# Routed attention and experts on one core: the first tiles' places moved among the products with v of the last turn but one, the first pair's preparation reordered, one transposition ahead of weights' sums

## The chip, the cores and the metric

The kernel runs on one core of one Trainium2 chip. The metric is the device time of one execution in microseconds; the kernel before takes 699.37 us (median of three runs, 699.08 to 699.43). The profile shows one execution with a span of 698.3 us and a mean granted TensorE clock of 0.990.

Five engines matter here. In the profile PE is TensorE's matmuls and PEld its weight loads, DVE is VectorE, ACT is ScalarE, POOL is GpSimd, and SP is the engine that issues most loads.

## The reference

An attention block in which a query sees only the keys of its own cluster, and then a layer of eight experts in which each row goes to one expert.

```python
# attention: q, k, v are (4, 8, 768, 64), centroids (8, 16, 64)
q_n = q / (norm(q) + 1e-06); k_n = k / (norm(k) + 1e-06); c_n = centroids / (norm(centroids) + 1e-06)
q_assign = argmax(einsum('bhsd,hcd->bhsc', q_n, c_n)); k_assign = argmax(einsum('bhsd,hcd->bhsc', k_n, c_n))
scores = scale * matmul(q, k.T)
scores = where(q_assign[..., :, None] == k_assign[..., None, :], scores, -1e9)
attn = exp(scores - max); attn = attn / (sum(attn) + 1e-09)
x = (attn @ v) as rows of 512, 3072 of them
# experts: w_gate (512, 8), w1 (8, 512, 1024), w2 (8, 1024, 512)
expert_idx = argmax(x @ w_gate, axis=1); gate_w = softmax(x @ w_gate)[expert_idx]
# rows sorted by expert; for each expert e:  y = relu(x_e @ w1[e]) @ w2[e];  out = gate_w * y
```

## The kernel before

The attention is done in 16 turns, numbered 0 to 15; a turn treats one pair of heads of one batch. A turn has 12 units: two halves of the queries by six blocks of keys. In each turn TensorE first makes the scores of all 12 units, ScalarE takes their exponentials into `A`, VectorE adds these up into `T` (the denominators), and then TensorE multiplies all 12 with v. A small scheduler hangs other jobs on points of a turn: `at(n, 4, f)` after the scores of unit 4, `at(n, mid, f)` between scores and products with v, `at(n, end, f)` after these products.

```python
def score(u):
    ps = ps_s.tile([P, 2, 512], F32, name="sps")       # three such buffers
    # 2 matmuls with qk, 2 with the one-hot clusters ohT
    A[u] = ap.tile([P, 2, HS], F32, name="A")          # 12 such buffers
    nc.scalar.activation(A[u], ps[:, :, 0:HS], AF.Exp, scale=D**-0.5)
    if j == 1:   # T = A[u-1] + A[u]
        nc.vector.scalar_tensor_tensor(T[g, half], in0=A[u - 1], scalar=1e-9 / P, in1=A[u], ...)
    elif j > 1:
        nc.vector.tensor_tensor(T[g, half], T[g, half], A[u], op=ALU.add)
# ... (cut)
for n in range(-4, NTURN + 2):
    for i, x in enumerate(range(n * NB, (n + 1) * NB)):
        if 0 <= x < NU:
            score(x)
        run(n, i)
    run(n, mid)
    for x in range(n * NB, (n + 1) * NB):
        if 0 <= x < NU:
            attend(x)                                   # products with v
    run(n, end)
```

While the last turns run, the first tiles of rows for experts 0 and 1 are placed: of the rows of the first three batches, each gets a slot (`slots1`), one-hot matrices are made from it (`one_hots1`, on VectorE and GpSimd), 18 small matmuls turn these into row numbers (`tokens1`), four more spread them over the partitions (`spread1`), and GpSimd gathers the rows (`gather1`). `n + 2` below is turn 14.

```python
n = NG - HP                                             # 16 - 4 = 12
at(n, end, choose, pl, front)
at(n + 1, mid, count, front)
at(n + 1, mid, slots1)
at(n + 1, mid, one_hots1, 0)
at(n + 1, end, one_hots1, 1)
at(n + 2, 4, tokens1)
at(n + 2, 8, spread1)
at(n + 2, 8, gather1, 0)
at(n + 3, mid, gather1, 1)
at(n + 3, mid, turn_rows1, 0)                           # L305 and L308 on VectorE
# ... (cut)
at(g, end, similar, g + 2); at(g, end, assign, g + 2)   # clusters of the turn after next
at(g, end, keep, g, 0, S); at(g + 1, mid, weigh, g)     # xb; sums' and gate's matmuls
at(NG, mid, first_half, 0, 0, FB // 4)                  # experts' first layer, from xu
```

The first pair's preparation, before turn 0: q and k are transposed on TensorE, the centroids `cn` are normalised and transposed (`blocks`, which fills `cblk`), and `similar` multiplies the two. `big` is a constant made on VectorE from an iota of GpSimd.

```python
# GpSimd: ident, cblk, first_c, first_e, wg, one_row, ohTs, then
nc.gpsimd.tensor_copy(wg[r, :, a, 0:E], wg_in[r])       # needs the load of wg_in
# VectorE: cs2, cinv, cn, and then
nc.gpsimd.iota(part_i, ...)
nc.vector.tensor_scalar(part_i, part_i, ...)            # then 5 small steps to big
# turn(0, 0): 4 transposes of q, 4 of k, copies to qk by VectorE (q) and ScalarE (k)
# blocks():   1 transpose of cn, 2 copies to cblk by VectorE
# turn(0, 1): 2 of q, 2 of k into one bank pair, one copy by ScalarE:
nc.scalar.copy(qk[g][:, :, 512:S], ps[:, 0 : 2 * n * P].rearrange("p (w s) -> p w s", w=2))
# put(0): four copies by ScalarE, four scalings by VectorE, into ohT
```

The experts' part begins with the tiles placed early; later full groups use seven products in place of eight (`sums_w1`, `sums_x` make the sums for them on VectorE).

```python
gather_of(groups[0]); adds[0](); gather_of(groups[1])
for f in sums_w1(groups[1]):                            # four sums of weights, L400 and L401
    f()
g = groups[0]
g["xT"] = p1.tile([P, DB, CAP], F32, name="xu", bufs=1)
divide_rows(g); turn_of(g)                              # L305 and L308, to xu
layer2(groups1[1])                                      # L386
layer1(g, (0, FB // 2)); layer1(g, (FB // 2, FB))       # L321, from xu
```

Of the kernel before, what the change touches and what calls it, by code (L numbers as in the profile page):

```python
# [8 lines left out]
F32 = mybir.dt.float32  # L9
BF16 = mybir.dt.bfloat16  # L10
I32 = mybir.dt.int32
AX = mybir.AxisListType.X
AF = mybir.ActivationFunctionType
ALU = mybir.AluOpType
# [6 lines left out]
NB = 12  # L21
# [164 lines left out]
def kernel(  # L186
# [243 lines left out]
    def sums_w1(g):  # L430
        t = pools["sums"].tile([P, 4, KH, F // 2], F32, name="w1s")
        g["w1s"] = [t[:, i] for i in range(4)]
        return sums_a(g["w1s"], *a_of1(g))
# [302 lines left out]
    with ExitStack() as actx:  # L736
# [55 lines left out]
        nc.scalar.dma_start(out=wg_in, in_=moe_w_gate.rearrange("(a p) e -> p a e", p=P))  # L792
        make_identity(nc, ident)
        nc.vector.tensor_copy(ident_b, ident)
        def idle(ps, n):

            for i in range(n):
                nc.tensor.matmul(ps[:, 0:P], lhsT=ident, rhs=ident, start=True, stop=True)  # L798
# [46 lines left out]
        for a in range(2):  # L845
            nc.vector.tensor_scalar(cn[:, a, :], csb, scalar1=cinv[:, 0:1], scalar2=None, op0=ALU.mult)


        part_i = consts.tile([P, 1], I32)
        nc.gpsimd.iota(part_i, pattern=[[0, 1]], base=0, channel_multiplier=1)  # L850
        nc.vector.tensor_scalar(
            part_i, part_i, scalar1=4, scalar2=1, op0=ALU.arith_shift_right, op1=ALU.bitwise_and
        )
        big = consts.tile([P, 2, 2], F32)
        nc.vector.tensor_copy(big[:, 1, 0:1], part_i)
        nc.vector.tensor_scalar_mul(big[:, 1, 0:1], big[:, 1, 0:1], BIG)
        nc.vector.tensor_scalar(big[:, 0, 0:1], big[:, 1, 0:1], scalar1=-1.0, scalar2=BIG, op0=ALU.mult, op1=ALU.add)
        for a in range(2):
            nc.vector.tensor_scalar_mul(big[:, a, 1:2], big[:, a, 0:1], -1.0)

        def blocks():
            cps = bank()
            nc.tensor.transpose(cps[:, 0:P], cn.rearrange("p a d -> p (a d)"), ident)
# [7 lines left out]
        def turn(g, piece):  # L871

            if piece == 0:
                qk[g] = qkp.tile([P, 2, S], F32, name="qk")
            n = NQ - 4 if piece else 4
            ps = wide().rearrange("p a c -> p (a c)")
            for i in range(2 * n):
                w, j = divmod(i, n)
                nc.tensor.transpose(
                    ps[:, i * P : (i + 1) * P], rows[g, "qk"[w]][:, 4 * piece + j].rearrange("p a d -> p (a d)"), ident  # L880
                )
            if piece == 0:
                apart(
                    nc.vector.tensor_copy(qk[g][:, 0, 0:512], ps[:, 0:512]),
                    nc.scalar.copy(qk[g][:, 1, 0:512], ps[:, 512:1024]),
                )
            else:
                nc.scalar.copy(qk[g][:, :, 512:S], ps[:, 0 : 2 * n * P].rearrange("p (w s) -> p w s", w=2))

        def turn_blocks(g):  # L890

# [50 lines left out]
        def places(half, a):  # L942

            return slice(half * 32, half * 32 + 32), slice(a * D, a * D + 32), slice(half * HS, (half + 1) * HS)
# [13 lines left out]

        def put(g):

            t, oh = sims.pop(g), ohTs[g % 2]
            ohT[g] = oh
            for half in range(2):
                for a in range(2):
                    i, r, cols = places(half, a)
                    k = slice(D + half * 32, D + half * 32 + 32)
                    nc.scalar.copy(oh[r, 0, cols], t[i])
                    nc.vector.tensor_scalar(
                        oh[r, 1, cols], t[k], scalar1=big[k, a, 0:1], scalar2=big[k, a, 1:2], op0=ALU.mult, op1=ALU.add
                    )  # L970


        A, T, O = {}, {}, {}
# [6 lines left out]
        def score(u):  # L980
            g, half, j = where(u)
            qs = slice(half * HS, (half + 1) * HS)
            ks = slice(j * P, (j + 1) * P)
            ps = ps_s.tile([P, 2, 512], F32, name="sps")
            for a in range(2):
                r = slice(a * D, (a + 1) * D)
                nc.tensor.matmul(ps[:, a, 0:HS], lhsT=qk[g][r, 1, ks], rhs=qk[g][r, 0, qs], start=True, stop=False)  # L987
            for a in range(2):
                r = slice(a * D, (a + 1) * D)
                nc.tensor.matmul(ps[:, a, 0:HS], lhsT=ohT[g][r, 1, ks], rhs=ohT[g][r, 0, qs], start=False, stop=True)  # L990
            A[u] = ap.tile([P, 2, HS], F32, name="A")
            nc.scalar.activation(A[u], ps[:, :, 0:HS], AF.Exp, scale=D**-0.5)  # L992
            if j == 1:
                T[g, half] = tp_.tile([P, 2, HS], F32, name="T", bufs=4)
                nc.vector.scalar_tensor_tensor(
                    T[g, half], in0=A[u - 1], scalar=1e-9 / P, in1=A[u], op0=ALU.add, op1=ALU.add
                )
            elif j > 1:
                nc.vector.tensor_tensor(T[g, half], T[g, half], A[u], op=ALU.add)  # L999

        def attend(u):
            g, half, j = where(u)
            if j == 0:
                O[g, half] = ps_o.tile([P, 512], F32, name="O")
            a_ = A.pop(u)
            for a in range(2):
                nc.tensor.matmul(  # L1007
                    O[g, half][a * D : (a + 1) * D, 0:HS], lhsT=rows[g, "v"][:, a, j, :], rhs=a_[:, a, :],
                    start=(j == 0), stop=(j == NQ - 1),
                )  # L1010
# [92 lines left out]
        def at(n, part, f, *a):  # L1103
            jobs.setdefault((n, part), []).append((f, a))
# [7 lines left out]
        at(3, end, place_consts2)  # L1112
        at(-4, mid, turn, 0, 0)
        at(-4, mid, load_next)
        at(-4, mid, blocks)
        at(-4, end, turn, 0, 1)
        at(-3, mid, similar, 0)
        at(-3, mid, assign, 0)
        at(-3, mid, assign2, 0)
        at(-3, mid, put, 0)  # L1120
        at(-2, end, idle_of, 20)
        at(-1, end, turn_blocks, 1)
        for f in (similar, assign, assign2):
# [62 lines left out]
        n = NG - HP  # L1186
        at(n, end, choose, pl, front)
        at(n + 1, mid, count, front)
        at(n + 1, mid, slots1)
        at(n + 1, mid, one_hots1, 0)  # L1190
        at(n + 1, end, one_hots1, 1)
        at(n + 2, 4, tokens1)
        at(n + 2, 8, spread1)
        at(n + 2, 8, gather1, 0)
        at(n + 3, mid, gather1, 1)
        at(n + 3, mid, turn_rows1, 0)

# [32 lines left out]
        def run(n, part):  # L1230
            for f, a in jobs.get((n, part), ()):
                f(*a)
# [4 lines that stand above are left out]
                    score(x)  # L1237
                run(n, i)
            run(n, mid)
            for x in range(n * NB, (n + 1) * NB):  # L1240
                if 0 <= x < NU:
                    attend(x)
            run(n, end)


# [86 lines left out]
    def turn_of(g):  # L1332
        if "xT" not in g:
            g["xT"] = pools["wk"].tile([P, DB, CAP], F32, name="xgT")
        turn_rows(g)
# [31 lines left out]
    adds[0]()  # L1367
    gather_of(groups[1])
    groups[0]["w"], groups[1]["w"] = weights[1], w_s
    for f in sums_w1(groups[1]):  # L1370
        f()
    g = groups[0]
    g["xT"] = p1.tile([P, DB, CAP], F32, name="xu", bufs=1)
    divide_rows(g)
    turn_of(g)
    layer2(groups1[1])
    gather_of(groups[2])
    groups[2]["xT"] = p1.tile([P, DB, P], F32, name="xT2", bufs=1)
# [107 lines left out]
```

## Time and profile before

| | busy | share of the span |
|---|---|---|
| PE | 676.6 us | 97% |
| PEld | 439.3 us | 63% |
| DVE | 471.8 us | 68% |
| ACT | 310.8 us | 45% |
| POOL | 250.1 us | 36% |

The page of the profile has busy times by engine, the span in 40 slices of 17.46 us, the chain of work that ended last, and groups of instructions. Apart from the page the trace answers questions: who waited for whom, the instructions in order of time, and busy times by stretches. In a line of the timeline stand the start, the duration, the engine, the line of the kernel, the operation, what it writes and reads, and in brackets how long the engine was idle before it and what released it. Matmuls of float32 stand there in two records each. The turns 12, 13, 14 and 15 start their scores at 251.97, 271.79, 292.01 and 321.38 us of the span, and the experts' first layer starts at 341.38 us.

### The profile page before, as it was taken

The numbers are of one execution on the slowest core, as the hardware profiler recorded it, in microseconds if no ns is written. First come the engines' busy times: TensorE is split into PE (matmuls) and PEld (weight loads), VectorE is DVE, ScalarE is ACT, GpSimd is POOL, SyncE is SP. The second block draws the span as 40 slices with busy tenths as digits, with TensorE's granted clock in tenths as the row PEclk, the third lists the DMA queues.
The fourth block names the chain that finished last, engine by engine and source line by source line (L and its number), as shares of the span: only waits on it lengthen the run. The fifth ranks groups of instructions, "written<-read, shape, count | busy, mean of one in ns | idle before, by whom it ended". The sixth has DMA issues, their size and how long they took to land.

```text
span 698.3 us, 11976 instructions
## 1 busy us (share of the span) xinstructions
PE 676.6 (97%) x4603; PEld 439.3 (63%) x4603; DVE 471.8 (68%) x739; ACT 310.8 (45%) x470; POOL 250.1 (36%) x327
## 2 busy tenths in 40 slices
PE   8999999999999999879999999999999999999994
PEld 6454444444454444445666679878798787888761
DVE  5997788778897778985656558666765767554300
ACT  3888777777887777658111022212112111131100
POOL 4022222211222222138605773737353463313101
PEclk9999999999999999989999999999999999999997
DMA  7667774986869652412245259766775866768540
GB/s 141 90 92 104 139 151 86 164 158 125 138 72 174 92 91 23 51 24 56 42 124 170 51 181 303 275 236 215 256 272 178 299 202 243 256 213 309 162 138 20
DMA packets 149538, 106.71 MB, mean 153 GB/s; under 512 B 115553, under 2 KB 119649, under 8 KB 149474
## 3 DMA queue, kind: packets, MB, share of 16 engines
q1 hardware_dynamic: 135266, 77.41, 43.6%
q0 software_dynamic: 8640, 19.63, 13.5%
q10 hardware_dynamic: 5568, 8.83, 4.1%
q8 instruction: 38, 0.62, 0.4%
q14 instruction: 26, 0.21, 0.1%
HBM read 93.06 MB, written 13.30 MB: 152 GB/s over the span
## 4 chain that ended last, share of the span: by engine, by line
PE 70%; issue 15%; POOL 6%; DVE 5%; DMA 1%; ACT 0%; ACTq 0%; POOLq 0%; DVEq 0%
PE sps L987 17%; PE O L1007 16%; PE sps L321 9%; PE sps L498 8%; PE sps L386 6%; PE sps L520 5%; PE sps L990 4%; POOL xg L292 3%; POOL out_dram L341 2%; PE sps L1029 2%; DVE T L999 2%; PE sps L908 2%; PE sps L357 1%; DMA xg<-x_rows,g_idx 1%; PE sps L798 1%
## 5 line engine op out<-in xcount | busy, mean ns | idle before, releaser
L992 ACT ACTIVATE A<-sps 128x768 f32<-128x768 f32 x192 | 153.5, 812 | 32.4 <-PE sps L990 28.6
L987 PE MATMUL sps<-qk 64*128 64x384 f32 x768 | 159.9, 495 | 2.7 <-DVE sim L915 2.2
L292 POOL DMA_INDIRECT xg<-x_rows,g_idx x104 | 115.7, 1113 | 122.4 <-DVE xgT L308 82.4
L999 DVE TENSOR_TENSOR T<-T,A 128x768 f32<-128x768 f32 x128 | 122.7, 959 | 13.0
L1007 PE MATMUL O<-A,v_in 128*64 128x384 f32 x768 | 127.4, 488 | 0.0
L987 PEld LDWEIGHTS sps<-qk 64*128 64x128 f32 x768 | 68.1, 189 | 53.3 <-issue 43.1
L1007 PEld LDWEIGHTS O<-A,v_in 128*64 128x64 f32 x768 | 53.7, 137 | 67.7 <-issue 65.9
L990 PE MATMUL sps<-ohT 64*128 64x384 bf16 x384 | 64.0, 326 | 0.0
L341 POOL DMA_INDIRECT out_dram<-zo,s_idx x32 | 38.5, 1204 | 69.4 <-ACT zo L337 30.7
L386 PE MATMUL sps<-w,h_sb 128*128 128x512 f32 x144 | 63.1, 592 | 0.0
L321 PEld LDWEIGHTS sps<-xgT,w 128*128 128x128 f32 x448 | 51.0, 192 | 3.7 <-issue 3.7
L321 PE MATMUL sps<-xgT,w 128*128 128x128 f32 x448 | 51.3, 275 | 0.0
L1041 POOL COPY dens<-ls 128x12 f32<-128x12 f32 x16 | 3.7, 232 | 127.7 <-DVE ls L1037 127.7
L1060 POOL DMA_DIRECT2D x_rows<-xb x68 | 48.3, 719 | 2.0 <-issue 0.5
L386 PEld LDWEIGHTS sps<-w,h_sb 128*128 128x128 f32 x144 | 26.8, 190 | 30.6 <-issue 30.6
L926 POOL TENSOR_TENSOR sim<-sim,first_c 128x384 f32<-128x384 f32 x14 | 14.0, 1003 | 87.8 <-DVE sim L925 87.8
L955 ACT ACTIVATE ohT<-ohs,big 32x384 bf16<-32x384 bf16 x60 | 42.0, 700 | 0.8
L364 ACT COPY zc<-sps 32x512 f32<-32x512 f32 x24 | 13.9, 579 | 60.2 <-PE sps L357 60.0
L498 PEld LDWEIGHTS sps<-xs,w1s 128*128 128x128 f32 x288 | 36.0, 190 | 5.0 <-DVE xs L409 4.2
L337 ACT COPY zo<-sps 128x512 f32<-128x512 f32 x12 | 7.0, 586 | 71.0 <-PE sps L386 65.2
L498 PE MATMUL sps<-xs,w1s 128*128 128x144 f32 x288 | 37.9, 288 | 0.0
L331 ACT ACTIVATE h_sb<-sps 128x512 f32<-128x512 f32 (+1 forms) x18 | 9.6, 578 | 60.2 <-PE sps L321 60.2
(261 smaller groups left out, 949.6 us busy)
## 6 DMA issues: line engine op xcount, KB each, us to landing
w<-in_moe_w_dram SPq DMA_DIRECT2D x28, 2048.0 KB, 9.2
w<-in_moe_w_dram ACTq DMA_DIRECT2D x16, 512.0 KB, 4.5
v_in<-in_v_dram SPq DMA_DIRECT2D x16, 384.0 KB, 3.8
q_in<-in_q_dram SPq DMA_DIRECT2D x60, 96.0 KB, 4.2
k_in<-in_k_dram SPq DMA_DIRECT2D x60, 96.0 KB, 5.6
x_rows<-xb POOLq DMA_DIRECT2D x60, 96.0 KB, 6.1
xg<-x_rows,g_idx POOLq DMA_INDIRECT x104, 3.5
x_rows<-pad SPq DMA_DIRECT2D x64, 3.0 KB, 2.2
```

Of the source, the lines that this page charges most:

```text
L292: nc.gpsimd.indirect_dma_start(out=g["xg"][:, n, :], out_offset=None, in_=x_q[0 : 4 * g["rows"], :], in_offset=bass.IndirectOffsetOnAxis(a ...
L321: nc.tensor.matmul(o, lhsT=g["w"][0][:, c, fb * P : (fb + 1) * P], rhs=g["xT"][:, c, :cols], start=(c == 0), stop=(c == DB - 1),)
L341: ins = nc.gpsimd.indirect_dma_start(out=out[:, :], out_offset=bass.IndirectOffsetOnAxis(ap=g["si"](j)[0:m], axis=0), in_=zo[0:m], in_offs ...
L386: nc.tensor.matmul(zp, lhsT=g["h"][:, fb, j * P : (j + 1) * P], rhs=g["w"][1][:, fb, :], start=(fb == 0), stop=(fb == FB - 1),)
L498: nc.tensor.matmul(o, lhsT=a[:, c, f * P : (f + 1) * P], rhs=b[:, c, :], start=(c == 0), stop=(c == KH - 1),)
L955: nc.scalar.activation(ohT[g][r, 1, cols], t[k], AF.Identity, scale=big[k, a, 0:1], bias=big[k, a, 1:2])
L987: nc.tensor.matmul(ps[:, a, 0:HS], lhsT=qk[g][r, 1, ks], rhs=qk[g][r, 0, qs], start=True, stop=False)
L990: nc.tensor.matmul(ps[:, a, 0:HS], lhsT=ohT[g][r, 1, ks], rhs=ohT[g][r, 0, qs], start=False, stop=True)
L992: nc.scalar.activation(A[u], ps[:, :, 0:HS], AF.Exp, scale=D**-0.5)
L999: nc.vector.tensor_tensor(T[g, half], T[g, half], A[u], op=ALU.add)
L1007: nc.tensor.matmul(O[g, half][a * D : (a + 1) * D, 0:HS], lhsT=rows[g, "v"][:, a, j, :], rhs=a_[:, a, :], start=(j == 0), stop=(j == NQ - 1),)
L1060: nc.gpsimd.dma_start(out=x_d[b * S + c0 : b * S + c1, quad, hp * 32 : (hp + 1) * 32].rearrange("(n t) d -> t n d", t=32), in_=xb[quad * 3 ...
```

## The change

It moves work of the last turns, of the start and of one place among the experts.

- The places: `slots1` and both `one_hots1` come after the products with v of turn 13, and so behind `similar` and `assign` of turn 15. `tokens1`, `spread1` and the first gather come among the products with v of turn 14, after the fourth and the ninth of the 12. To have VectorE free for them, the sums into `T` of units 3 to 11 of turn 14 are put off until after the gather's indices. The aim is that TensorE need not stand for the placing.
- The start: `big` is made first; `blocks` comes between the transposes of q and of k; the copy of the second piece is split between VectorE and ScalarE; two of ScalarE's four copies in `put` come after two exponentials of turn 0.
- The experts: the division and transposition of the first group's rows come before the four sums of weights of the next group.

The core of the diff, with cuts:

```diff
+        part_i = consts.tile([P, 1], I32)      # moved up with big, ahead of idle, cblk, ..., cn
+        nc.gpsimd.iota(part_i, pattern=[[0, 1]], base=0, channel_multiplier=1)
 # ... (cut)
+                if i == n and piece == 0:
+                    blocks()
                 nc.tensor.transpose(
-                    ps[:, i * P : (i + 1) * P], rows[g, "qk"[w]][:, 4 * piece + j]. ...
+                    ps[:, w * 512 + j * P : w * 512 + (j + 1) * P], rows[g, "qk"[w]][:, 4 * piece + j]. ...
             else:
-                nc.scalar.copy(qk[g][:, :, 512:S], ps[:, 0 : 2 * n * P].rearrange("p (w s) -> p w s", w=2))
+                for w, copy in enumerate((nc.vector.tensor_copy, nc.scalar.copy)):
+                    copy(qk[g][:, w, 512:S], ps[:, w * 512 : w * 512 + n * P])
 # put: the copies of the second half are put_q(0, 1)
+        at(0, 1, put_q, 0, 1)
 # score:
+            if g == NG - 2 and u % UG >= 3:
+                later_sums.append((u, A[u]))
+            else:
+                add_up(u, A[u])
 # ... (cut)
-        at(n + 1, mid, slots1)
-        at(n + 1, mid, one_hots1, 0)
+        at(n + 1, end, slots1)
+        at(n + 1, end, one_hots1, 0)
         at(n + 1, end, one_hots1, 1)
-        at(n + 2, 4, tokens1)
-        at(n + 2, 8, spread1)
-        at(n + 2, 8, gather1, 0)
+        at(n + 2, UG + 3, tokens1)
+        at(n + 2, UG + 8, spread1)
+        at(n + 2, UG + 8, gather1, 0)
+        at(n + 2, UG + 8, sums_of_later)
 # ... (cut)
-            for x in range(n * NB, (n + 1) * NB):
+            for i, x in enumerate(range(n * NB, (n + 1) * NB)):
                 if 0 <= x < NU:
                     attend(x)
+                run(n, NB + i)
 # ... (cut), the experts:
-    for f in sums_w1(groups[1]):
-        f()
     g = groups[0]
     g["xT"] = p1.tile([P, DB, CAP], F32, name="xu", bufs=1)
     divide_rows(g)
     turn_of(g)
+    for f in sums_w1(groups[1]):
+        f()
     layer2(groups1[1])
```

## The prediction

> **What bounds the kernel now.** I began with the page: busy shares and the span in slices.
>
> ```profile
> PE   8999999999999999879999999999999999999994
> DVE  5997788778897778985656558666765767554300
> PEclk9999999999999999989999999999999999999997
> ```
>
> TensorE is full nearly everywhere; only the first slice and slices 17 and 18 (279 to 314 us) are not, and the granted clock dips there too. So time is to be had only where TensorE stands or runs slowly. Who it waited for, over the whole span:
>
> ```profile
> PE sps L691 <- POOL oh_c L681: 3.4, 1, 3.4
> PE sps L987 <- DVE sim L915: 2.2, 1, 2.2
> PE sps L908 <- DVE cblk L866: 1.7, 1, 1.7
> PE sps L321 <- DVE xu L308: 1.5, 1, 1.5
> ...
> PE sps L987 <- DVE tv L700: 0.4, 1, 0.4
> ```
>
> The change aims at all five. Turn 13 beside turn 14, by busy times in stretches (length, PE, PEld, DVE, ACT, POOL, clock, DMA share, GB/s), with a stretch after the long wait:
>
> ```profile
> 271.79:292.01 20.22, 20.22 (x158) 10.14 (x156) 18.68 (x31) 15.37 (x22) 4.70 (x8) 1.00 0.48 43
> 292.01:321.38 29.37, 23.38 (x171) 11.32 (x167) 20.48 (x43) 15.04 (x21) 13.92 (x16) 0.88 0.21 40
> ...
> 304.00:306.00 2.00, 2.00 (x10) 0.91 (x8) 1.83 (x6) 0.81 (x1) 0.00 (x0) 0.50 0.02 4
> ```
>
> Turn 14 takes 9 us more than turn 13, 6 of them idle, the rest at a clock of 0.50. TensorE's timeline shows it:
>
> ```profile
> 298.68 0.38 PE L691 MATMUL sps<-oh_c,oh_r 128*128 128x8 bf16 x9
> 302.48 0.38 PE L691 MATMUL sps<-oh_c,oh_r 128*128 128x8 bf16 x9 [3.42 <-POOL oh_c L681]
> 302.79 1.65 PE L987 MATMUL sps<-qk 64*128 64x384 f32 x4
> 304.23 0.53 PE L990 MATMUL sps<-ohT 64*128 64x384 bf16 x2
> 304.55 1.49 PE L987 MATMUL sps<-qk 64*128 64x384 f32 x4
> ```
>
> After the wait a unit of scores takes 1.6 us; in turn 13 it takes 0.81.
>
> The start, from the chain that ended last:
>
> ```profile
> 7.11 0.21 POOL wg L825
> ...
> 7.38 0.14 POOL part_i L850
> ...
> 8.51 0.60 DVE qk L884
> ...
> 9.62 0.85 PE sps L908 x8
> ```
>
> The constant `big` waits for a load of the gate's weights that it doesn't need, and VectorE's copies wait behind `big`.
>
> [...] 0.50 after the 3.42 us idle, for some 5.5 us, while the wait of 2.2 us at 294 us left the clock at 1.00. [...] So I follow VectorE by adding durations in program order. [...] The two `oh_c` took 1.50 us beside VectorE's one-hots (0.75 each); for the gathers it isn't plain (1.53 and 1.71 us beside sums, 0.94 later). I use it for the range.
>
> **Part 1, the places.** Times are those of the trace before, without the earlier start.
>
> TensorE. Scores of turn 14 start at 292.01. `similar` of turn 15 is now read by VectorE at once, so its buffer is free and the 2.2 us wait goes; 12 units take 9.89 us as in turn 13 (271.79 to 281.68): 301.90. `weigh` 1.11 (chain): 303.01. Products with v are 7.89 for 12, 0.66 each; four make it 305.64. The 18 place matmuls take 2 x 0.31 (302.48 to 302.79): 306.26. Five products: 309.55; the spread 0.18; three products: turn 15 starts at about 311.7 instead of 321.38.
>
> Is the placing ready? VectorE has `cnt_f` done at 291.0, and `similar` to `ohs` takes 4.56 from 292.1 (turn 13: 271.91 to 276.47): 296.7. The slots take 3.03 (291.01 to 294.04): 299.7. Two rounds of one-hots, 1.38 (294.04 to 295.42) and 1.34 (299.97 to 301.31): 302.4. GpSimd's second pair starts after its first, 299.9 + 1.5 + 1.2 = 302.6. TensorE asks at 305.6, 3 us later: no wait. Two sums and the denominators' transpose bring VectorE to 305.2, before the place matmuls end at 306.3; `hlb` follows at once, and the spread at 309.6 finds it. So TensorE wins 321.38 - 311.7 = 9.7 us here.
>
> Not all of it stays. VectorE's indices are done at 309.75 + 1.05 = 310.8. Then come the eight postponed sums: 3.0 for three (311.81 to 314.81) and 5.1 for five (283.37 to 288.49): 318.9. That is ahead of what needs them: the exponential that reuses unit 3's buffer comes at about 315, its sum ends at 311.9; `weigh` of turn 14 is due at 311.7 + 9.89 = 321.6. `xb` takes 1.0: 319.9. The ten sums of turn 15 then run without a pause, 10.3: 330.2. TensorE has finished turn 15's products at 321.6 + 1.11 + 7.89 = 330.6, and `weigh` of turn 15 at 331.7. But the experts' first layer needs `xu`:
>
> ```profile
> 335.39 1.51 DVE L305 TENSOR_TENSOR xg<-xg 128x1152 f32<-128x1152 f32 x1
> 336.93 1.38 DVE L308 STREAM_TRANSPOSE xu<-xg 128x1152 f32<-128x1152 f32 x1
> ```
>
> From the last sum to L305 is 0.8 (334.60 to 335.39), to the end of L308 another 2.85: 330.2 + 3.65 = 333.85. TensorE waits about 2.1 us for VectorE, and its first layer starts at 333.9 instead of 341.4. **Part 1: 7.5 us**, of 9.7 that TensorE alone would give. The gathers start 1.3 us earlier, at 310.9; nine in 12.3 us and 3.5 to land put the last at about 326, in time.
>
> **Part 2, the start.** `big` moves into VectorE's free time before 3.13 us, where it waits for the centroids. `cn` is there at 6.56; its transpose follows q's and is done at 6.9, `cblk` (0.45) at 7.4. q's copy (0.68) then ends at 8.1, that of the second piece (about 0.4, from 0.68 for 512 columns) at 8.5, and `similar` starts at about 8.6 instead of 9.62: 1.0 us. The 40 idle matmuls behind it and VectorE's chain to `ohT` move with it. In turn 0 some is lost: k of turn 1, whose last load is issued at about 13.3 with 3.5 us to land, may hold VectorE until 16.8 where it could start at 16.4, and its transpose of `sim` releases TensorE at 23.14. The two postponed copies of `put` let the first exponential start 0.7 us sooner and delay the third by as much: nothing net. **Part 2: 0.8 us.**
>
> **Part 3, the sums of weights.**
>
> ```profile
> 384.00 0.68 DVE L371 TENSOR_TENSOR zo<-zc 32x512 f32<-32x512 f32 x1
> ...
> 388.13 1.22 DVE L401 TENSOR_TENSOR w1s<-w,w1s 128x1024 f32<-128x1024 f32 x1
> 390.12 0.84 DVE L308 STREAM_TRANSPOSE xu<-xg 128x640 f32<-128x640 f32 x1
> ```
>
> Four sums (384.61 to 389.26) go behind L305 and L308. The last of the five gathers is issued at 381.62, and with 3.5 us lands at 385.1, so `xu` is there at about 386.9, before TensorE is done with L386 at 389.6. Its wait of 1.5 us goes; the sums end at 391.6 and aren't read before 407. **Part 3: 1.5 us.**
>
> **The sum.** 7.5 + 0.8 + 1.5 = 9.8; 699.4 - 9.8 = 689.6 us. Behind 391 us TensorE waits for no engine, and loads of weights follow the release of their buffers by TensorE, so the gain should reach the end.
>
> **Rivals.** (a) VectorE isn't a bound: it catches up sooner than I add, or the wait for `xu` is small. Then part 1 gives up to 9.7, and the kernel takes 687.4. Against it: VectorE has no gap from 310 to 334 us in my sum. (b) The new wait is longer: sums and gathers held up by each other, rows landing after 331, or a wait for `xu` beyond 3.4 us, with the experts' first layer at half clock. A clock of 0.50 for 5.5 us costs about 2.7 us, the longer wait 1 to 2: 693 to 694. For it: VectorE's chain is tight, and the first gathers took 1.5 to 1.7 us beside sums. Against: 12.3 us for nine is measured with sums beside the first ones, and 5 us are to spare. (c) The gain is taken back among the experts by GpSimd or transfers, which the chain shows from 557 us on: 697 or more. Against it: TensorE's timeline has no gap there that an engine ended, and the matmuls end at 688.2, 10 us before the span.
>
> **Range and chances.** Prediction 689.6. (a) sets the low end, 687.4, and a mild (b) the high end, 692.0. Faster by over 2% would need 685.4, more than all the waits hold: 0.03. Slower by over 2% needs a wait nobody shows: 0.01. Within 2%: 0.96.
>
> **What would show it.** Right: the waits for `oh_c`, for `sim` at turn 14 and for `xu` of 128x640 are gone; turn 14's products and places end about 9.7 us sooner; no 0.50 clock there; one new wait of about 2 us, L321 for `xu` of 128x1152; `similar` at about 8.6. Wrong: that wait missing, or above 3.4 us with half clock after it; `weigh` of turn 14 or exponentials of turn 15 waiting for `T`; gaps in TensorE after 400 us that weren't there.

## The result, and the profile after

The changed kernel takes 693.92 us (median of four runs, 692.79 to 695.03); the kernel before, beside it, 699.23 us. The ratio is 0.9924, with a 95% interval of 0.9904 to 0.9944. A second series gave 693.07 us and 0.991 (0.9897 to 0.9923). So the change wins some 5.3 to 6.8 us of the 9.8 predicted, and the time lies above the range of 687.4 to 692.0 us.

The profile after is of the run of 692.79 us, with a span of 691.1 us. The page's slices, to set beside those of before:

```profile
PE   8999999999999999999899999999999999999994
DVE  6987788788898778879666269566765667564200
PEclk9999999999999999999999999999999999999998
```

The dent of slices 17 and 18 is gone from PE and from the clock. A smaller dent stands in slice 19 (counted from 0, 328 to 346 us). Who TensorE waited for, over the span, with the sum of the waits, their number and the longest:

```profile
PE sps L321 <- DVE xu L308: 2.0, 1, 2.0
PE sps L498 <- issue: 1.6, 1, 1.6
PE sps L811 <- POOL ident masks.py:199: 1.4, 1, 1.4
PE sps L386 <- ACT hs L331: 0.6, 1, 0.6
PE sps L911 <- POOL b1off_i L252: 0.6, 1, 0.6
PE sps L911 <- ACT A L1002: 0.4, 1, 0.4
```

The waits for `oh_c`, `sim`, `tv` and `cblk` are gone. The wait for `xu` at L321 is now the one for 128x1152 that the prediction foretold, 2.0 us for 2.1. The second line was foretold by nothing: 1.6 us at L498, put down to "issue", that is, to nothing that the profile sees.

Turn 14 from its first scores to those of turn 15, by busy times (columns as before):

```profile
292.26:312.18 19.92, 19.92 (x170) 9.98 (x167) 15.06 (x39) 14.89 (x21) 9.32 (x14) 1.00 0.23 42
```

19.92 us with no idle time and a full clock, where it was 29.37 with 6 of them idle. The first layer follows, in TensorE's timeline:

```profile
334.24 15.76 PE L321 MATMUL sps<-xu,w 128*128 128x288 f32 x64 [1.98 <-DVE xu L308]
```

It starts at 334.24 instead of 341.38, so 7.14 us have been won by then. What is missing is missing elsewhere, behind this point and at the start. Here is the new wait, in the timeline of all engines behind 390 us:

```profile
391.17 0.41 SPq L236 DMA_DIRECT2D w<-in_moe_w_dram  x1
391.17 0.49 DVE L329 TENSOR_SCALAR h_sb<-sps 128x320 f32<-128x320 f32 x1 [3.78 <-PE sps L321]
391.19 0.95 POOL L292 DMA_INDIRECT xg<-x_rows,g_idx  x1 [0.30 <-issue]
...
397.63 1.36 DVE L305 TENSOR_TENSOR xg<-xg 128x1152 f32<-128x1152 f32 x1 [5.97 <-DMA xg<-x_rows,g_idx]
...
401.49 0.73 PE L498 MATMUL sps<-xs,w1s 128*128 128x144 f32 x4 [1.64 <-issue]
```

and the same place in the kernel before:

```profile
398.01 0.95 POOL L292 DMA_INDIRECT xg<-x_rows,g_idx  x1 [0.30 <-issue]
...
400.07 0.41 SPq L236 DMA_DIRECT2D w<-in_moe_w_dram  x1
...
400.60 1.38 DVE L305 TENSOR_TENSOR xg<-xg 128x1152 f32<-128x1152 f32 x1
```

L305 divides the rows of the second group, and needs the last gather of that group (L292). Before, the gather had a start of 2.06 us on the 2 MB load of weights (L236), and its rows were there by 400.60, 2.6 us after the issue, without a wait. Now both are issued within 0.02 us, and L305 waits 5.97 us, until 6.4 us after the issue. L308 and the sums into `xs` follow (L408, L409), and TensorE's first product with `xs` comes 1.64 us late. The wait stands under "issue", but the chain to it is plain from VectorE's lines.

Why the load caught up with the gather: both come sooner than before, the load by 8.90 us and the gather by 6.82. The load waits for a buffer that TensorE's L321 releases (SyncE stands 15.7 us for it before and 14.0 after, and issues the load at 400.07 and 391.17), and L321 no longer waits for `xu`. GpSimd's gathers go on in their own order. The trigger of the load came forward by 2.08 us more than the gather that the load now disturbs.

### The profile page after: what moved, and what is told of

The parts are those of the page before. It is cut to its first block, busy times and chain, and to the rows that moved or that the text cites. A ratio compares the mean times of both kernels' runs of the same rounds, so it can differ in the third digit from the quotient of the medians.

```text
span 691.1 us, 11981 instructions
## 1 busy us (share of the span) xinstructions
PE 674.3 (98%) x4603; PEld 439.6 (64%) x4603; DVE 471.8 (68%) x740; ACT 310.7 (45%) x470; POOL 253.0 (37%) x327
## 4 chain that ended last, share of the span: by engine, by line
PE 74%; issue 14%; POOL 7%; DMA 2%; DVE 1%; ACT 1%; ACTq 0%; POOLq 0%; DVEq 0%
PE O L1034 17%; PE sps L997 17%; PE sps L321 9%; PE sps L498 8%; PE sps L386 7%; PE sps L520 5%; POOL xg L292 5%; PE sps L1000 4%; PE sps L1056 2%; POOL out_dram L341 2%; PE sps L911 2%; PE sps L357 1%; PE sps L811 1%; DMA xg<-x_rows,g_idx 1%; DMA wg_in<-in_moe_w_gate_dram 1%
## 5 line engine op out<-in xcount | busy, mean ns | idle before, releaser
L292 POOL DMA_INDIRECT xg<-x_rows,g_idx x104 | 120.0, 1154 | 116.6 <-DVE xgT L308 81.9
L997 PE MATMUL sps<-qk 64*128 64x384 f32 x768 | 157.1, 487 | 0.1
L386 PE MATMUL sps<-w,h_sb 128*128 128x512 f32 x144 | 63.1, 592 | 0.0
L321 PEld LDWEIGHTS sps<-xgT,w 128*128 128x128 f32 x448 | 51.0, 192 | 3.7 <-issue 3.7
L321 PE MATMUL sps<-xgT,w 128*128 128x128 f32 x448 | 51.3, 275 | 0.0
L386 PEld LDWEIGHTS sps<-w,h_sb 128*128 128x128 f32 x144 | 26.8, 190 | 30.6 <-issue 30.6
L498 PEld LDWEIGHTS sps<-xs,w1s 128*128 128x128 f32 x288 | 36.0, 190 | 6.7 <-DVE xs L409 4.2
L498 PE MATMUL sps<-xs,w1s 128*128 128x144 f32 x288 | 37.8, 288 | 1.6 <-issue 1.6
```

Of the source, the lines that this page charges most:

```text
L292: nc.gpsimd.indirect_dma_start(out=g["xg"][:, n, :], out_offset=None, in_=x_q[0 : 4 * g["rows"], :], in_offset=bass.IndirectOffsetOnAxis(a ...
L321: nc.tensor.matmul(o, lhsT=g["w"][0][:, c, fb * P : (fb + 1) * P], rhs=g["xT"][:, c, :cols], start=(c == 0), stop=(c == DB - 1),)
L386: nc.tensor.matmul(zp, lhsT=g["h"][:, fb, j * P : (j + 1) * P], rhs=g["w"][1][:, fb, :], start=(fb == 0), stop=(fb == FB - 1),)
L498: nc.tensor.matmul(o, lhsT=a[:, c, f * P : (f + 1) * P], rhs=b[:, c, :], start=(c == 0), stop=(c == KH - 1),)
```

## The experiments

The first theory, from the two traces: part 1 came as predicted; part 3's 1.5 us are given back by the collision of load and gather; part 2 is lost somewhere at the start; and in part of the runs the clock falls to half behind the wait for `xu`. The rivals: part 1 is worth less than it looks and the rest is as predicted; or the gain is lost in the long stretch behind 400 us (rival (c) of the prediction).

### The changed kernel once more, and each part by itself

`again` is the changed kernel without an edit.

> The changed kernel once more, to see what parts its runs, which lay at 692.8 and at 695.0 us. Theory A: the 2.2 us between them are half clock in one stage, begun by one of the two new waits of TensorE (2.0 us for xu, 1.6 us ahead of L498); a run at 695 shows a stretch of about 4 us at a clock of 0.50 right behind one of them, and mean clock 0.993 instead of 0.996. Theory B: it is the start[...]; then the idle matmuls and the transposes differ and the rest is the same. Expected: runs between 692.5 and 695.5 us, in two heaps.

Measured: 693.07 us (692.29 to 694.83). Four of the five runs lie between 692.29 and 693.41, one at 694.83: two heaps, as expected. The profile is of a run of 692.29 us and doesn't show what parts them; `no_part3` below does.

`part1_only` is the kernel before with part 1 of the diff, `put`'s copies kept together:

```diff
-        at(n + 2, 4, tokens1)
-        at(n + 2, 8, spread1)
-        at(n + 2, 8, gather1, 0)
+        at(n + 2, UG + 3, tokens1)
+        at(n + 2, UG + 8, spread1)
+        at(n + 2, UG + 8, gather1, 0)
+        at(n + 2, UG + 8, sums_of_later)
 # and the slots and one-hots of the same part
```

> The kernel before with the places' part of the change alone. Theory A: part 1 carries the whole gain, 7.0 to 7.5 us where no half clock follows the wait for xu and about 5 us where it does; the waits for oh_c and sim in turn 14 are gone, and the wait for xu of 128x1152 is 2.0 us. Rival: the three parts add up to what the changed kernel gains only together, and part 1 alone gives 4 us or less.

Measured: 692.44 us (694.2, 692.42, 692.45, 692.39) beside 699.42, ratio 0.9899 (0.9885 to 0.9913). Part 1 alone gives 7.0 us, more than the whole change in its first series. In its trace L321 starts at 333.86, 7.52 us sooner than before: the prediction's 7.5. (The profiled run of before took 700.01 us, 0.6 above its median.)

`part3_only` is the kernel before with the last part of the diff alone:

```diff
-    for f in sums_w1(groups[1]):
-        f()
     divide_rows(g)
     turn_of(g)
+    for f in sums_w1(groups[1]):
+        f()
```

> The kernel before with the sums of weights moved, and nothing else. Theory A: the wait for xu of 128x640 (1.5 us) goes, a wait of about 1.6 us ahead of L498 comes, and the time is the same within 0.4 us. Rival: the collision of load and gather comes only with the earlier turns; then this part alone brings 1.5 us.

Measured: 699.9 us, ratio 1.0006 (1.0000 to 1.0013): nothing, and by no means 1.5 us. The first lines of TensorE's waits (the places are those of before in it, with their waits):

```profile
PE sps L691 <- POOL oh_c L681: 3.4, 1, 3.4
PE sps L987 <- DVE sim L915: 2.2, 1, 2.2
PE sps L498 <- issue: 1.5, 1, 1.5
```

The wait of 1.5 us for `xu` is out of the list, and one of 1.5 us at L498 is in it. The load is issued at 398.43 and the group's last gather at 398.46, and L305 waits 5.83 us for the rows. Beside the 400.07 and 398.01 of before, the load comes 1.64 us sooner and the gather 0.45 us later: two of GpSimd's issues take 1.75 and 1.97 us beside the moved sums, where before only one took 1.94. So part 3 makes its own loss, without help from the other parts.

`no_part3` is the changed kernel with that edit taken back.

> Changed kernel with the four sums of weights ahead of the division and transposition again, as before. Theory A: part 3's 1.5 us are given back at L498, so time is the same within 0.4 us; the wait for xu of 128x640 (1.5 us) is back, and the 1.6 us ahead of L498 are gone. Rival (the wait at L498 comes from something else, part 3 is worth its 1.5 us): time rises by 1.5 us.

Measured: 693.93 us (692.46 to 695.13), ratio 0.9911 (0.9896 to 0.9925). TensorE's waits for `xu` are two again, 3.5 us together, and L498 doesn't wait. From the other side too, part 3 is worth nothing.

One stretch of the traces shows it without the scatter of the times: from L321's first product with the rows of 128x1152 to the first product of L520, a later layer. It takes 88.28 us before (341.38 to 429.66), and 88.09 in `part3_only` (341.47 to 429.56): 0.19 us won where 1.5 were predicted. From L520's first product to the end of the span the kernel before, the changed one and all eight kernels from `again` to `busy_wait` take 268.6 to 268.7 us. So the rival that the gain is lost in the long stretch behind 400 us holds for the one wait at L498 and for nothing behind 430 us.

### The load behind the gather

`load_later` is the changed kernel with the weights' load held back until the second group's last gathered rows have landed, by a transfer of one element out of them, ahead of it in the same queue:

```diff
+    held2 = pools["wk"].tile([1, 1], F32, name="held2", bufs=1)
+    nc.sync.dma_start(out=held2, in_=groups[1]["xg"][0:1, NJ * 4, DB * 32 : DB * 32 + 1])
     fetch1_of(2)
```

> Changed kernel, the load of weights for the third group kept back until the last gathered block of the second group has landed. Theory A: that load, which now starts in the same moment as the last gather's issue, keeps the rows from landing (6.4 us instead of under 2.6); kept back, the 1.6 us wait ahead of L498 goes, and time falls by 1.3 to 1.8 us against the changed kernel. Rival: the gathers are late by themselves, since GpSimd issues them beside the moved sums (1.75 and 1.96 us for two of them); then the wait stays and time changes by under 0.5 us.

Measured: 692.24 us (690.9 to 692.88), ratio 0.9894 (0.988 to 0.9909), 0.8 us less than `again` in the same series; I had expected 1.3 to 1.8 less, and the two profiled runs do differ by 1.39 us (690.9 and 692.29). L498 doesn't wait, and VectorE's L305 comes at 393.56:

```profile
390.98 0.95 POOL L292 DMA_INDIRECT xg<-x_rows,g_idx  x1 [0.30 <-issue]
...
393.56 1.38 DVE L305 TENSOR_TENSOR xg<-xg 128x1152 f32<-128x1152 f32 x1 [2.10 <-DMA xg<-x_rows,g_idx]
...
395.69 0.41 SPq L236 DMA_DIRECT2D w<-in_moe_w_dram  x1
```

That is 4 us sooner than in the changed kernel. With the load out of the way the same gather, issued 0.21 us sooner, lands 2.6 us after its issue, which shows the collision to be the cause and not only its companion. From L321's first product to L520's first it is 86.52 us (334.03 to 420.55), 1.76 less than before: without the collision part 3 gives what was predicted for it, and a little more.

### The wait for xu, and the clock behind it

The prediction has VectorE as the bound ahead of `xu`, with eight postponed sums in its way. `two_sums` lets two of the eight run earlier, behind `tokens1`:

```diff
-        def sums_of_later():
-            for x in later_sums:
+        def sums_of_later(m=NB):
+            for x in later_sums[:m]:
                 add_up(*x)
+            del later_sums[:m]
+        at(n + 2, UG + 3, sums_of_later, 2)
```

> Changed kernel, two of the eight postponed sums already between the place matmuls and the spread, where VectorE stands for 2.3 us. Theory A: VectorE sets the start of the experts' first layer, so the 2.0 us wait for xu goes almost whole and time falls by 1.7 to 2.1 us; if the half clock of the slower runs hangs on that wait, the two heaps become one as well, and the median falls by up to 3 us. Rival: the sums delay the indices and the gathers, and xu waits for its rows: no gain.

Measured: 690.66 us (690.37 to 691.78), ratio 0.9874 (0.986 to 0.9888). The first lines of TensorE's waits:

```profile
PE sps L498 <- issue: 1.6, 1, 1.6
PE sps L811 <- POOL ident masks.py:199: 1.4, 1, 1.4
PE sps L386 <- ACT hs L331: 0.6, 1, 0.6
```

The wait for `xu` is gone, and the median is 2.4 us under that of `again` for a wait of 2.0. No run lies near 695.

`both` has the edits of `two_sums` and `load_later`.

> The changed kernel with two postponed sums moved to VectorE's gap, and the load of weights kept back behind the gather. Theory A: the two gains add up, since they lie in different stages: 1.5 us below the kernel with the two sums alone, so 689.0 to 689.5 us, and neither wait is left. Rival: the kept back load comes late for its own use and costs what it brought: 690.5 us.

Measured: 689.13 us (688.86 to 689.46), ratio 0.9851 (0.9839 to 0.9864). This is the best time that was measured beside a kernel before of 699.4, 4 us under the changed kernel, and it is inside the range that the prediction gave the change. That is no confirmation of the prediction: it had counted the wait of 2 us for `xu` as staying, and `both` removes that one too.

The runs of the changed kernel fall in two heaps, some 693 and some 695. The one profile of `no_part3` is of a run of 695.13 us, and shows why, in stretches of two microseconds behind the wait of 2.0 us:

```profile
334.00:336.00 2.00, 1.16 (x4) 0.87 (x5) 0.69 (x1) 0.00 (x0) 1.70 (x2) 0.83 0.39 21
336.00:338.00 2.00, 2.00 (x6) 1.43 (x5) 0.91 (x3) 0.00 (x0) 1.39 (x3) 0.50 0.25 47
338.00:340.00 2.00, 2.00 (x9) 1.50 (x8) 1.62 (x7) 0.00 (x0) 2.00 (x3) 0.82 0.33 68
340.00:342.00 2.00, 2.00 (x10) 1.58 (x9) 0.27 (x2) 0.95 (x3) 2.00 (x5) 1.00 0.53 83
```

The granted clock is the third column from the right. It is 0.50 for some 3.5 us, behind a wait of 2.0 us; in the same stretches of the changed kernel's profile (a run of 692.79) it is 1.00:

```profile
336.00:338.00 2.00, 2.00 (x10) 1.57 (x9) 1.48 (x7) 0.00 (x0) 1.70 (x2) 1.00 0.30 68
```

Ten records of products in two microseconds instead of six. `busy_wait` tells whether it is the standing idle that does it. TensorE's wait is filled with eight products that nobody reads (`n` is NG there):

```diff
+        at(n, mid, idle_of, 8)
         at(n, mid, first_half, 0, 0, FB // 4)
```

> The changed kernel with 8 idle products of the identity (16 records, 1.9 us) ahead of the experts' first layer, so that TensorE works while it waits for xu. Theory A: the half clock behind the wait comes from standing idle; it is gone, no run lies at 695, and all runs lie between 692.2 and 693.5 us, though xu is there no sooner. Theory B (the half clock has another origin): runs at 695 stay as frequent as in the changed kernel (3 of 9 so far).

Measured: 691.2 us (690.65 to 692.31), ratio 0.9885 (0.987 to 0.9899). Its TensorE timeline:

```profile
332.19 2.05 PE L811 MATMUL sps<-ident 128*128 128x128 f32 x16
334.26 10.91 PE L321 MATMUL sps<-xu,w 128*128 128x288 f32 x44
```

L321 starts no sooner than in the changed kernel (334.26 and 334.24), yet no run lies near 695. By itself that is weak: where seven of 19 runs lie there (counted below), four without one come about by chance one time in six. With `two_sums` and `both`, where TensorE doesn't stand there at all, it is 13 runs without one, so that the standing is well supported as the cause; that idle products alone prevent the half clock is only suggested. The median is below what I expected of this kernel, for another reason: L498's wait is gone from its profile too. There the last gather was issued at 390.78, 0.4 us ahead of the load at 391.19, and L305 came at 395.52. One more of the gathers fell ahead of the sums of weights there (issued at 379.02, 0.98 us long), and so the later ones came sooner. That some tenths of a microsecond in the order of issue decide 1.6 us fits the collision, and it means that the 0.45 us by which part 3 delays the gather belong to the loss: the load's coming forward by 1.64 us alone would have left the gather a start of 0.42, as much as it has here.

### The start

`part2_only` is the kernel before with part 2 alone, `part2_again` the same kernel in another series, and `no_part2` the changed kernel without part 2.

> The kernel before with part 2 of the change alone (constants, centroids' block and copies at the start, and the two postponed copies of put). My prediction gave part 2 0.8 us: then 698.5 to 698.8 beside 699.4. The traces of the kernels so far suggest that little of it stays: the idle matmuls ahead of the first transpose take 4.6 to 5.9 us from run to run, with nothing to spare behind them now, and ScalarE's copy of k's second piece waits for VectorE's copy of q: then -0.3 to +0.2 us, 699.1 to 699.6. In the trace: similar of turn 0 at 8.6 by the prediction, at 8.2 to 9.4 by the second theory; the first scores at most 0.3 us sooner.

> The changed kernel with part 2 taken back. If part 2 was worth 0.8 us, this takes 0.8 us more than the changed kernel, about 694.0; if it is worth nearly nothing, 692.4 to 693.5, with the same wait of about 2.0 us for xu and of 1.6 us at L498, and single runs at 695 where the clock falls to half behind the wait for xu.

Measured: 715.47 us beside 717.1 (ratio 0.9988, 0.9965 to 1.0012), and 705.62 us (0.9835, 0.9802 to 0.9868). In this series and those that follow every kernel, the one before too, took some 15 us more, which the traces show to be lost behind 380 us, and the times scattered by up to 1%. So they are set only beside that series' own, they can't decide between 0.8 us and nothing, and the start is read from the traces.

> The kernel before with part 2 alone, once more, since the first series of this kernel was taken where every kernel, that before too, stood some 15 us behind 395 us. In its trace the first unit's scores began 0.70 us sooner than before, but the scores of the seventh only 0.09 us sooner. If this holds, the time is 0 to 0.3 us less than before; by my prediction 0.8 us less.

Measured: 715.87 us beside 715.21, ratio 1.0007 (0.9987 to 1.0027).

The start has a piece that no kernel here is sure of: 13 idle products (26 records) on TensorE, ahead of the first transposition. In the kernel before:

```profile
1.43 4.58 PE L798 MATMUL sps<-ident 128*128 128x128 f32 x26 [1.43 <-POOL ident masks.py:199]
5.84 0.60 PE L879 MATMUL sps<-ident,q_in 128*128 128x128 f32 x4
...
9.62 0.85 PE L908 MATMUL sps<-qk,cblk 128*32 128x384 f32 x8 [1.70 <-DVE cblk L866]
```

and in `part2_again`:

```profile
1.43 5.92 PE L810 MATMUL sps<-ident 128*128 128x128 f32 x26 [1.43 <-POOL ident masks.py:199]
7.14 0.81 PE L880 MATMUL sps<-ident,q_in 128*128 128x128 f32 x4
...
9.49 1.48 PE L910 MATMUL sps<-qk,cblk 128*32 128x384 f32 x8 [0.57 <-DVE qk L885]
```

The same 26 records take 4.58 or 5.92 us. Start times from TensorE's timelines, all kernels but those that change the start again (us; the eighth unit's scores are a mark of how far turn 0 has come, and the expectations call it the seventh, counting from nought):

| kernels | first q transposition | `similar` of turn 0 | eighth unit |
|---|---|---|---|
| without part 2: before, part1_only, part3_only, no_part2 | 5.84, 6.97, 7.14, 6.30 | 9.62, 9.47, 9.66, 9.66 | 22.34, 22.19, 22.38, 22.38 |
| with part 2: two_sums, part2_only, again, load_later, both | 5.92, 5.96, 6.24, 6.33, 6.39 | 8.24, 8.29, 8.38, 8.48, 8.54 | 22.13, 22.25, 22.18, 22.31, 22.26 |
| with part 2: busy_wait, after, both_again, no_part3, part2_again | 6.71, 6.82, 7.13, 7.13, 7.14 | 8.87, 8.97, 9.30, 9.53, 9.49 | 22.46, 22.57, 22.90, 23.13, 23.09 |

Without part 2 `similar` comes at about 9.6 whatever the idle products take, since the wait for `cblk` swallows the difference. With part 2 that wait is gone, and `similar` follows the idle products, 2.1 to 2.4 us behind the first transposition: at 8.24 to 8.54 where they are short, as the prediction's 8.6 had it. At the eighth unit the ten with part 2 have a mean of 22.53 and the four without one of 22.32: part 2 does not pay at all on average. And what is lost at the start stays lost: beside the changed kernel the eighth unit comes 0.39 us sooner in `again` and 0.56 later in `no_part3`, and L321 0.35 sooner and 0.60 later (333.89, 334.24, 334.84).

And even where `similar` comes 1.3 us sooner, at most 0.2 us reach the eighth unit. Two causes were tried. ScalarE's copy of k's second piece waits for VectorE's copy of q's, though they touch different elements. Changed kernel, ScalarE's timeline:

```profile
9.18 0.37 ACT L891 COPY qk<-sps 128x256 f32<-128x256 f32 x1 [0.60 <-DVE qk L891]
```

`both_apart` is `both` with these two declared independent, as the two copies of the first piece are; `both_apart_10` has 10 idle products instead of 13 besides.

```diff
-                for w, copy in enumerate((nc.vector.tensor_copy, nc.scalar.copy)):
-                    copy(qk[g][:, w, 512:S], ps[:, w * 512 : w * 512 + n * P])
+                apart(*(
+                    copy(qk[g][:, w, 512:S], ps[:, w * 512 : w * 512 + n * P])
+                    for w, copy in enumerate((nc.vector.tensor_copy, nc.scalar.copy))
+                ))
```

> The best version so far (two of the postponed sums later, the weights' load behind the gather: 689.1 us), with the two copies of the second q and k piece declared independent, as those of the first piece are. If ScalarE's wait for VectorE's copy costs the start 0.6 us, similar of turn 0 is 0.6 us shorter and the time 688.5 to 688.8; if the start is bound by what VectorE does after it, 689.0 to 689.3.

> The same with 10 instead of 13 idle matmuls ahead of the first transpose. If these idle matmuls bind the start, they end 0.7 to 1.3 us sooner and the time falls by up to 0.8 us, to 687.9 to 688.5; [...]no change, 688.5 to 689.3[...].

> The best version with the copies of the second piece declared independent, once more. Its trace had the seventh unit's scores 0.59 us sooner than before and 0.51 us sooner than without this. If the start's gain reaches the end, 688.4 to 688.8 beside 689.1 for the version without; if it is taken back later, 689.0 to 689.4.

Measured: 706.89 us (0.9866), 705.46 us (0.9846) and, again, 706.33 us (0.9865, 0.9827 to 0.9904). In the traces `similar` takes 1.08 us instead of 1.48, and the eighth unit comes at 21.75, 21.75 and 21.94; in `two_sums`, whose `similar` starts as early (8.24), it comes at 22.13. The ten idle products took 4.63 us in 20 records, no less than 26 records took elsewhere (4.58 and 4.66), so three products fewer bought nothing in this one trace. The time of `both_apart_10` is 1.4 us under that of `both_apart`, but not by way of the start: their eighth units are level, and the traces part between 416 us and L520's first product (435.71 and 434.48); the mean clock of 300 to 500 us is 0.96 in `both_apart` and 0.97 in `both_apart_10`.

The other cause is the split of `put`. ScalarE's timeline in `part2_again`:

```profile
15.32 1.04 ACT L977 COPY ohT<-ohs 32x384 bf16<-32x384 bf16 x2 [5.24 <-DVE ohs L942]
16.77 1.62 ACT L1001 ACTIVATE A<-sps 128x768 f32<-128x768 f32 x2 [0.41 <-PE sps L999]
18.41 1.03 ACT L977 COPY ohT<-ohs 32x384 bf16<-32x384 bf16 x2
19.47 2.21 ACT L1001 ACTIVATE A<-sps 128x768 f32<-128x768 f32 x3
```

From the first copy to the end of the fifth exponential it is 6.36 us. `part2_put` has the four copies together again (`put_q(g, 1)` behind `put_q(g, 0)` in `put`, and the later call removed), and so does `both_put`, on top of `both_apart`.

> Part 2 alone, but with put's four copies together again. In the trace of part 2 alone, ScalarE starts put's copies 0.30 us sooner than before, and ends its fifth exponential 0.31 us later: it stands 0.41 us between the first two copies and the first exponential. If the split of put is what loses the gain, the third exponential comes about 0.6 us sooner than in part 2 alone and similar of turn 1 at about 19.3 instead of 19.48, seventh unit at 22.05; if something else binds there (TensorE itself, or VectorE's sums), both stay where they are. In the time 0.2 to 0.3 us, at the edge of what can be measured.

> The same with put's four copies together. If ScalarE's order is what loses the rest of part 2, another 0.2 us: 688.2 to 688.6, and similar of turn 1 at about 18.8. If not, no difference.

ScalarE's timeline in `part2_put`:

```profile
14.40 2.10 ACT L978 COPY ohT<-ohs 32x384 bf16<-32x384 bf16 x4 [5.41 <-DVE ohs L942]
16.52 3.62 ACT L1002 ACTIVATE A<-sps 128x768 f32<-128x768 f32 x5
```

5.74 us, 0.6 less. With the split, ScalarE stands 0.41 us between the first copies and the first exponential, and five exponentials take 1.62 + 2.21 = 3.83 us in two pieces and 3.62 in one. The eighth unit comes at 21.96 (22.18 and 22.31 in `again` and `load_later`, whose `similar` starts at much the same time), and at 21.61 in `both_put`: 0.73 us sooner than before, close to the 0.8 predicted, where the idle products are short. In time: 715.59 us (1.0003, 0.9977 to 1.0028), and 706.61 us (0.987, 0.9831 to 0.9908), both too scattered to show it.

Two last kernels, `both` and `both_put` in one series:

> The version with two of the postponed sums later and the weights' load behind the gather, once more, to stand beside the next kernel in one series: 0.986 of before, as at first (0.9851).

> The same with the start mended (copies of the second piece declared independent, put's four copies together). Its trace had the seventh unit of scores at 21.61, that of the version without at 22.26. If the start's gain reaches the end, this takes about 0.6 us less than both_again in the same series; if it is taken back behind the start, no difference of more than 0.2 us.

Measured: 706.76 and 706.5 us (0.987 and 0.9865). The eighth unit is at 22.90 and 22.46, with long idle products in both (5.89 and 5.92 us), so that even the mended start comes no sooner than before here (22.34). The lead is still 0.46 us at 417 us of the span (L498 at 417.31 and 416.85), and 0.15 at L520's first product (435.75 and 435.60). The times differ by 0.26 us where each scatters by 1.4 to 1.7: what the mended start is worth at the end, in series like the earlier ones, stays open.

## Why the prediction was wrong, step by step

**Part 1 was right.** Turn 14 takes 19.92 us, the prediction's 311.7 - 292.0 = 19.7. No wait for `oh_c`, for `sim` or for the exponentials came; the new wait of L321 is 1.98 us for 2.1; L321 starts at 333.86 in `part1_only`, 334.24 in the changed kernel, for 333.9. In time it is 7.0 us where it stands alone, for 7.5; against the profiled run of before, 0.6 above its median, it would be 7.6 in the runs at full clock. Following VectorE by adding durations in program order held over 40 us: in the changed kernel the gather's indices are done at 311.3 (predicted 310.8), the postponed sums at 319.4 (318.9), turn 15's sums at 330.5 (330.2) and `xu` at 334.1 (333.85).

**Part 3 was wrong, by all of its 1.5 us.** The failed step is "Its wait of 1.5 us goes; the sums end at 391.6 and aren't read before 407": I looked at what the moved sums feed, and not at what a sooner L321 triggers. "Loads of weights follow the release of their buffers by TensorE, so the gain should reach the end" is the same mistake, turned into a reassurance: that the load follows is what brought it onto the gather. In its place the load was issued at 398.43 instead of 400.07, beside the last gather, L305 waited 5.83 us for the rows, and TensorE 1.5 us at L498. Shown by `part3_only` (nothing won, the wait changed place), `no_part3` and `load_later`. It is rival (c) in kind, though (c) looked for it from 557 us on and at 697 us or more; I argued it down with "TensorE's timeline has no gap there", and a timeline of before can't show a gap that the change opens. The sign of being wrong that I had named, "gaps in TensorE after 400 us that weren't there", is what came. How load and gather share the transfers was not shown; what the runs show is the gather's 6.4 us beside the load and 2.6 us ahead of it.

**Part 2 was mis-sized: 0.8 us predicted, at most 0.2 us in a good start, and -0.2 us on average.** Three terms are missing. The idle products were taken at their 4.58 us of one trace, at the short end of 4.58 to 5.92, and with part 2 there is no wait left to hide them. "That of the second piece (about 0.4 ...) at 8.5, and `similar` starts at about 8.6" took the two copies as side by side; `similar` did start there, but took 1.48 us instead of 0.85, 0.40 of it for ScalarE's copy, which `both_apart` freed. And "the two postponed copies ... nothing net" cost 0.6 us on ScalarE, of which some 0.2 reached the eighth unit.

**The clock was not priced in.** Rival (b) had the half clock, but tied it to "a wait for `xu` beyond 3.4 us", the length of the one wait that had a clock of 0.50 behind it in the trace of before (3.42 us at L691); the wait was 2.0, so that its "693 to 694" was met partly by luck. Seven of 19 runs of the changed kernel, `again`, `no_part3` and `part1_only` lie at 694.2 to 695.1 where the others of the same kernel lie at 692.3 to 693.4; the profiles of two of the seven show 0.50 behind a wait of 2.0 us, and no run of `two_sums`, `both` or `busy_wait`, where the wait is gone or filled, lies 2 us above its kernel's median. (`load_later`, which keeps the wait, isn't counted: its four runs scatter from 690.9 to 692.88 without clear heaps.) In the traces the half clock costs 1.66 us: from L321's first product to L520's first it is 89.94 us in `part1_only` and in `no_part3`, 88.28 before. The seven runs lie 2.1 us above the others on average; in seven of 19 that makes 0.8 us, and more in the first series, where it was two of four. That the clock can fall behind only 2.0 us of standing is measured here (0.50 in `part1_only` and `no_part3`, 1.00 in the changed kernel and `again`, each behind a wait of 2.0 us). What decides in which runs it falls, and why the same 26 idle records at the start take 4.58 us in one trace and 5.92 in another, was not shown.

**The sum.** In the profiled runs L321 starts 7.14 us sooner than before (7.5 for part 1, less some 0.2 for a later start), the stretch to L520's first product gives 0.09 (88.28 and 88.19), and nothing changes behind it: 7.2 us, the difference of the spans. The predicted 9.8 had 1.5 for part 3 and 0.8 for part 2 besides, and these two with the later start are nearly all that is missing. The medians show 5.3 and 6.8 us and not 7.2, since the profiled run of before lies 0.6 above its median and the runs at half clock take 0.8 on average.

## What to carry to other kernels

When a change lets an engine release a buffer sooner, list what that release triggers, and look at what is in flight at the new time: a large load that starts beside a small gather that is waited for can take back the whole gain (1.5 us in `part3_only`). A stage that had slack hid its variable parts; once the slack is removed, price them at their mean and not at the one value that a trace shows. And a stand of TensorE cost more than its length here in part of the runs (2.0 us of standing, and 1.66 us lost at half clock behind it); filling it with idle products may then be worth a trial even where they bring nothing closer.

## What the runs showed of the hardware that I had not expected

- A clock of 0.50 for some 3.5 us behind a wait of only 2.0 us, in the profiles of `part1_only` and `no_part3` and not in those of the changed kernel, `again` and `load_later`, which have the same wait; the wait of 2.2 us at 294 us of the kernel before left it at 1.00 in its profile.
- The rows of a gather issued at the same moment as a 2 MB load let L305 start 6.4 us after its issue, those of one with a start of 0.41 us 4.7 us after (`busy_wait`), and those of one with a start of 2.06 us were there within 2.6 us (the kernel before).
- At the start, the 128x384 TENSOR_TENSOR of VectorE on `sim` that begins while GpSimd copies to `to_quarters` took 0.91 us in `part2_only`, 0.73 in `part2_put` and 0.84 in `two_sums`, beside a copy of 0.60 us; in the kernel before, where none overlaps the copy, it took 0.56. In `both_apart` two overlap the copy: they took 0.56 and 0.78, and the copy 0.87.
- In the later series TensorE stood behind 395 us for what the profile calls "issue", product by product, in every kernel whose profile I have of them. `both` in its first series and `both_again`, 395 to 425 us:

```profile
395.00:425.00 30.00, 30.00 (x224) 27.05 (x223) 21.28 (x29) 7.93 (x14) 18.34 (x18) 1.00 0.78 259
```

```profile
395.00:425.00 30.00, 18.42 (x104) 13.99 (x103) 9.44 (x16) 4.23 (x7) 17.02 (x18) 0.77 0.36 115
```

The same stretch of the span, 30.00 us busy and 18.42, with a mean clock of 1.00 and 0.77; at 373 us the two are 0.74 us apart (L386 at 373.36 and 374.10), about what they are apart at the start. What TensorE lacked there the traces don't show. The kernels from `again` to `busy_wait` ran on two other chips than the later ones, so that the chip may be the reason; it wasn't tried.
